# Six of the sixteen q/k transposes of an attention + experts kernel moved from TensorE to DMA by way of DRAM

## The chip, the cores and the metric

One core of one Trainium2 chip runs the whole program. The metric is the device time of one execution in microseconds (us). A set of runs alternates the kernel before with the kernels under test on the same chip. The chip was not the same in every set, so a kernel is compared with the kernel before of its own set. A profile comes from one execution of each kernel. TensorE is the matmul engine, VectorE and ScalarE the elementwise engines, GpSimd issues DMAs that cast, and SyncE ("SP") issues plain and transposing DMAs.

## The reference

```python
# q, k, v: [8 batches, 8 heads, 576 tokens, 64]; causal window of 128, ALiBi bias
scores = scale * q @ k.T + bias           # masked outside 0 <= i-j < 128
attn = softmax(scores); x = attn @ v      # -> x [4608 tokens, 512]
P = sinkhorn(exp(x @ w_gate), 8 rounds)   # [4608, 8 experts]
out = sum_e P[:, e] * (relu(x @ w1[e]) @ w2[e])
```

Three stages follow each other: attention (batches 0 to 7, about 10 to 192 us), the Sinkhorn rounds with some work of expert 0, and the experts (from about 230 us to the end). During attention TensorE also does work of expert 0 for token groups that are ready. The code calls that `fill`; the amount is fixed.

## The kernel before

A score matmul needs q and k with the head dimension on the partitions, so both are transposed. `load_qk` brings q and k in with a cast to fp16, `turn` rearranges a half batch on VectorE, and `tr_unit` transposes two heads with six TensorE transposes into one PSUM bank, from which ScalarE (k) or VectorE (q) copies them out. A tensor (the k or q of one batch) takes four such groups.

```python
def tr_unit(b, nm, j, swap=0):
    tt = turned[nm]
    psT = aps.tile([P, RT, RP], FP16, ..., tag="pmm", bufs=pmm)   # one PSUM bank
    for r in range(RT):                                           # RT = 6, RP = 96
        nc.tensor.matmul(out=psT[:, r, :],
                         lhsT=tt[:, r, 2 * Dh * jj : 2 * Dh * jj + 2 * Dh],
                         rhs=ident[0:RP, 0:RP], is_transpose=True, ...)
    copy = nc.scalar.copy if (nm == "k") != bool(swap) else nc.vector.tensor_copy
    copy(out=(KTs if nm == "k" else QTs)[b % 2][:, j, :]..., in_=psT...)

for i, (b, kb) in enumerate(blocks):        # five blocks of 128 tokens a batch
    if i < first_i: continue                # batches 0, 1, part of 2: a hand-written ORDER
    units = [(b + 1, nm, kb - 1) for nm in ("k", "q")]     # if kb >= 1: the NEXT batch
    pt0, mask0 = scores(b, kb, 0)           # score matmuls, exp on ScalarE
    gates(done); done = finish2(i - 2)      # transposes of x, store of x
    for u in units[: len(units) // 2]: tr_unit(*u)         # the k group
    fill(1)
    if turning: turn(b + 1, kb // 2, "k")
    mask0()
    pt1, mask1 = scores(b, kb, 1)
    xsbs[i - 1] = finish(i - 1)             # attention matmuls of the block before
    mask1(); fill(2)
    for u in units[len(units) // 2 :]: tr_unit(*u)         # the q group
    fill(1)
    if turning: turn(b + 1, kb // 2, "q")
    if kb == 0: load_v(b + 1)
    if kb == 3: load_qk(b + 2)
```

The score PSUM tile has one buffer, so the scores of one half can only be written when the exponential has read those of the half before.

The softmax here doesn't subtract the row's maximum and nothing guards it: scores larger than these inputs give would overflow.

## Time and profile before

| | |
|---|---|
| time, median | 1020.05 us (1018.93 to 1022.19, 4 runs) |
| profiled span | 1016.9 us |
| TensorE matmul busy | 98% of the span |
| batches 3 to 6, first score of 3 to first score of 7 | 72.6 to 165.4 us, 92.8 us |

The head of the page: span, and busy time of TensorE, its share and its instructions.

```profile
span 1016.9 us, 22579 instructions
...
PE 994.6 (98%) x9245; PEld 808.9 (80%) x9245; DVE 820.5 (81%) x1272; ACT 650.5 (64%) x1193; POOL 214.2 (21%) x224
```

The table by stretch, cut at the first score matmul of batches 3, 4, 5, 6 and 7. Columns: the stretch, its length, then busy us (and instructions) of TensorE, its weight loads, VectorE, ScalarE and GpSimd, then the granted clock, the mean DMA share and GB/s. (The prediction cut the same stage some 6 us later, from 78.5 us.)

```profile
core 0: us, PE busy (x) PEld busy (x) DVE busy (x) ACT busy (x) POOL busy (x), PEclk, DMA share, GB/s
72.60:96.70 24.10, 22.76 (x255) 12.71 (x252) 16.09 (x34) 16.20 (x29) 7.01 (x10) 1.00 0.81 101
96.70:119.80 23.10, 22.08 (x255) 12.45 (x252) 15.96 (x33) 15.76 (x29) 6.96 (x9) 1.00 0.85 101
119.80:142.00 22.20, 21.87 (x252) 12.28 (x250) 15.09 (x31) 16.01 (x28) 6.12 (x9) 1.00 0.87 104
142.00:165.40 23.40, 22.90 (x258) 12.75 (x256) 15.92 (x34) 16.69 (x30) 2.52 (x3) 1.00 0.35 60
```

TensorE is busy 89.6 of 92.8 us in batches 3 to 6; VectorE (63.1) and ScalarE (64.7) have room. The list of waits for these 92.8 us (line, tile, what it waited for, total us, times, longest) shows how little TensorE is held by others:

```profile
PE psS_2_0_1444 L265 <- ACT pt_1_1_1420 L276: 0.7, 1, 0.7
PE psS_3_0_1919 L265 <- ACT pt_2_1_1885 L276: 0.4, 1, 0.4
PE psS_3_0_1517 L265 <- ACT pt_2_1_1483 L276: 0.4, 1, 0.4
```

These are the three longest of nine, scores that wait for an exponential to free their PSUM tile; all nine sum to 3.0 us. Then one k group in the timeline (start, duration, engine, line, operation): six weight loads and six matmuls of L226, the first weight load of the next matmul 0.27 us after the group's first, and the copy out of PSUM on ScalarE.

```profile
87.58 0.33 PEld L226 LDWEIGHTS <-kp_1_1475 96*128 96x128 f16 x6
87.64 0.42 PE L226 MATMUL psT_k_2_1536<-ident,kp_1_1475 96*128 96x96 f16 x6
87.85 0.10 PEld L129 LDWEIGHTS <-w1t_122 128*128 128x128 f16 x1
...
88.17 0.65 ACT L235 COPY KT_75<-psT_k_2_1536 128x576 f16<-128x576 f16 x1
```

### The profile page before, as it was taken

The page shows a single profiled execution, that of the slowest core. Times are in us where ns is not written, and L with a number is a line of the kernel's source. Part 1 is how long each engine was busy: PE and PEld are TensorE (multiplying, and loading weights), DVE is VectorE, ACT ScalarE, POOL GpSimd, SP SyncE. Part 2 cuts the span into 40 slices and gives each one's busy share as a digit, 9 for nine tenths or more (in the row PEclk, how much of TensorE's full clock was granted, in tenths as well). Part 3 has the DMA queues.
Part 4 walks back from the last instruction along what each step waited for, and adds up shares of the span by engine and source line. Part 5 has one row for each costly group of instructions (what it writes and reads, how often), then busy time and mean ns, then how long its engine had stood idle before and what let it go on. Part 6 is the DMA issues. An engine that isn't in the chain of part 4 may idle for free. (4 is left out here: it accounts for less than half of the span.)

```text
span 1016.9 us, 22579 instructions
## 1 busy us (share of the span) xinstructions
PE 994.6 (98%) x9245; PEld 808.9 (80%) x9245; DVE 820.5 (81%) x1272; ACT 650.5 (64%) x1193; POOL 214.2 (21%) x224
## 2 busy tenths in 40 slices
PE   7899999999999999999999999999999999999997
PEld 4555555447888788888888888888888888888886
DVE  4677676587999897888888988888889988888886
ACT  6766776557999766666666556566656566666562
POOL 7423310110333221111112111111112112222222
PEclk9999999999999999999999999999999999999999
DMA  9997971391977874444447667444437645655546
GB/s 166 196 132 92 101 90 60 73 217 56 218 160 161 200 145 94 100 98 94 102 104 146 135 146 143 101 95 95 94 94 144 126 95 139 147 148 138 136 94 135
DMA packets 126936, 127.35 MB, mean 125 GB/s; under 512 B 44112, under 2 KB 104816, under 8 KB 126832
## 3 DMA queue, kind: packets, MB, share of 16 engines
q0 software_dynamic: 94784, 60.58, 43.2%
q1 hardware_dynamic: 31728, 65.07, 20.5%
q8 instruction: 72, 1.18, 0.5%
q10 hardware_dynamic: 320, 0.26, 0.1%
q14 instruction: 32, 0.26, 0.1%
HBM read 112.90 MB, written 16.66 MB: 127 GB/s over the span
## 5 line engine op out<-in xcount | busy, mean ns | idle before, releaser
L129 PEld LDWEIGHTS <-w1t_122 128*128 128x128 f16 x288 | 25.9, 97 | 26.9 <-issue 1.9
L743 PEld LDWEIGHTS <-w1t_3295 128*128 128x128 f16 x288 | 28.2, 98 | 5.1 <-issue 1.7
L743 PEld LDWEIGHTS <-w1t_3277 128*128 128x128 f16 x288 | 28.2, 98 | 4.6
L743 PEld LDWEIGHTS <-w1t_8419 128*128 128x128 f16 x288 | 28.1, 98 | 4.4 <-issue 0.3
L743 PEld LDWEIGHTS <-w1t_5217 128*128 128x128 f16 x288 | 28.1, 98 | 3.8 <-issue 0.3
L743 PEld LDWEIGHTS <-w1t_7883 128*128 128x128 f16 x288 | 28.2, 98 | 3.6 <-issue 0.3
L743 PEld LDWEIGHTS <-w1t_10819 128*128 128x128 f16 x288 | 28.2, 98 | 3.6 <-issue 0.3
L743 PEld LDWEIGHTS <-w1t_4035 128*128 128x128 f16 x256 | 25.1, 98 | 2.9
L204 POOL DMA_DIRECT2D vsb_79<-in_v_dram x20 | 17.1, 864 | 38.1 <-PE psN_1_1888 L318 5.9
L204 POOL DMA_DIRECT2D vsb_80<-in_v_dram x20 | 17.3, 870 | 34.8 <-PE psN_1_1486 L318 5.7
L576 POOL PARTITION_ALL_REDUCE ca_sb<-cs_sb x8 | 3.1, 389 | 63.0 <-DVE cs_sb L573 62.9
L265 PEld LDWEIGHTS <-KT_76 64*128 64x128 f16 (+1 forms) x160 | 5.4, 96 | 13.4 <-issue 12.1
L618 ACT ACTIVATE acc_lo<-acc_lo,Pe_sb 128x512 f32<-128x512 f32 (+1 forms) x24 | 14.8, 616 | 0.0
L265 PEld LDWEIGHTS <-KT_75 64*128 64x128 f16 (+1 forms) x160 | 5.2, 97 | 11.8 <-issue 10.4
L85 POOL DMA_DIRECT2D out_dram<-acc_lo x12 | 13.5, 1527 | 0.0
L343 PEld LDWEIGHTS <-xT 128*128 128x128 f16 x144 | 6.1, 96 | 5.1 <-issue 2.9
L871 POOL DMA_DIRECT2D acc_lo<-st_1_0_3878 x1 | 1.2, 1243 | 34.4 <-ACT st_1_0_3878 L870 34.4
L743 PEld LDWEIGHTS <-ws_2_4353 128*128 128x128 f16 x72 | 7.0, 98 | 1.5 <-issue 0.7
L743 PEld LDWEIGHTS <-ws_1_3597 128*128 128x128 f16 x72 | 7.0, 97 | 1.3
L85 POOL DMA_DIRECT2D out_dram<-acc_hi x6 | 5.7, 1575 | 9.7 <-DVE acc_hi L861 9.7
L898 DVE TENSOR_TENSOR acc_lo<-acc_lo 128x512 f32<-128x512 f32 x12 | 7.7, 685 | 0.0
L743 PEld LDWEIGHTS <-ws_6_10891 128*128 128x128 f16 x72 | 7.0, 98 | 0.8
(4175 smaller groups left out, 3566.4 us busy)
## 6 DMA issues: line engine op xcount, KB each, us to landing
xTd<-xT SPq DMA_DIRECT2D x9, 512.0 KB, 4.5
out_dram<-acc_lo SPq DMA_DIRECT2D x12, 256.0 KB, 5.3
vsb_79<-in_v_dram POOLq DMA_DIRECT2D x16, 128.0 KB, 5.8
vsb_80<-in_v_dram POOLq DMA_DIRECT2D x16, 128.0 KB, 5.8
out_dram<-acc_lo SPq DMA_DIRECT2D x12, 128.0 KB, 3.7
out_dram<-acc_lo POOLq DMA_DIRECT2D x12, 128.0 KB, 7.4
w1t_122<-in_moe_w_dram POOLq DMA_DIRECT2D x2, 512.0 KB, 11.3
w2t_130<-in_moe_w_dram POOLq DMA_DIRECT2D x1, 1024.0 KB, 16.4
```

Of the source, the lines that this page charges most:

```text
L85: eng.dma_start(out=out[t0 : t0 + n, c0:c1], in_=t[n * c : n * c + n], **kw)
L129: nc.tensor.matmul(out=psh, lhsT=w1t[:, dt, P * ft : P * ft + P], rhs=x[:, dt, :], start=(dt == 0), stop=(dt == NDT - 1),)
L204: nc.gpsimd.dma_start(out=vsb[0:nk, kb, :, 0:Dh], in_=v[b, :, k0 : k0 + nk, :].rearrange("h s d -> s h d"),)
L265: nc.tensor.matmul(out=ps[0:nk, hh, jj, 0:nq], lhsT=KT[rows, 2 * half + jj, k0 : k0 + nk], rhs=QT[rows, 2 * half + jj, k0 : k0 + nq], star ...
L343: nc.tensor.matmul(out=psG, lhsT=xT[:, dt, P * blk : P * blk + P], rhs=wg_sb[:, dt, :], start=(dt == 0), stop=(dt == NDT - 1),)
L576: nc.gpsimd.partition_all_reduce(ca_sb, cs_sb, P, bass_isa.ReduceOp.add)
L618: nc.scalar.mul(acc(blk)[:, c], acc(blk)[:, c], Pe_sb[:, 0, blk : blk + 1])
L743: nc.tensor.matmul(out=ps[:, f, :], lhsT=a[:, kt, f0 : f0 + P], rhs=b[:, kt, :], start=(m in (1, 5) and f == 0 and kt == 0), stop=(kt == 1 ...
L871: nc.gpsimd.dma_start(out=quad(self.g, rh, ch), in_=st, accum_op=ALU.add)
L898: tt(out=t, in0=t, in1=quad(g, 1, 1), op=ALU.add)
```

## The change

The intent is to take transposes off the bounding engine. For six tensors (k of batches 4 to 7, q of 5 and 7), a casting DMA writes fp16 to DRAM as [576 tokens, 512], and one transposing DMA on SP's queue reads it into the finished K or Q tile. `tr_unit` and `turn` are dropped for them.

```diff
+        by_dma = {("k", b) for b in range(4, B)} | {("q", b) for b in range(5, B, 2)}
+        d16 = {nb: nc.dram_tensor(..., [S, HD], FP16, kind="Internal").ap() for nb in sorted(by_dma)}
         def load_qk(b: int):
+            for nm, src in (("k", k), ("q", q)):
+                if (nm, b) in by_dma:
+                    nc.gpsimd.dma_start(
+                        out=d16[nm, b].rearrange("s (h d) -> s h d", d=Dh),
+                        in_=src[b].rearrange("h s d -> s h d"),
+                    )
...
-                    units = [(b + 1, nm, kb - 1) for nm in ("k", "q")]
+                    units = [(b + 1, n, kb - 1) for n in ("k", "q") if (n, b + 1) not in by_dma]
+                if kb == 1:
+                    for nm, t in (("k", KTs), ("q", QTs)):
+                        if (nm, b + 1) in by_dma:
+                            nc.sync.dma_start(
+                                out=t[(b + 1) % 2], in_=d16[nm, b + 1], transpose=True
+                            )
...
-                if turning:
+                if turning and ("k", b + 1) not in by_dma:
                     turn(b + 1, kb // 2, "k")
...          (the same for q)
```

More of the change, by code (lines that the diff above doesn't have):

```diff
@@ L184 @@
         raw: dict = {}
-        def load_qk(b: int):
+        by_dma = {("k", b) for b in range(4, B)} | {("q", b) for b in range(5, B, 2)}
+        d16 = {
+            nb: nc.dram_tensor(f"{nb[0]}16_{nb[1]}", [S, HD], FP16, kind="Internal").ap()
+            for nb in sorted(by_dma)
+        }
+        def load_qk(b: int):
+            for nm, src in (("k", k), ("q", q)):
[4 more added lines that the diff above has]
+                    )
             for half in range(2):
@@ L189, in load_qk @@
                 for nm, src in (("k", k), ("q", q)):
+                    if (nm, b) in by_dma:
+                        continue
                     t = asb.tile(
@@ L519 @@
                 fill(1)
-                if turning:
+                if turning and ("q", b + 1) not in by_dma:
                     turn(b + 1, kb // 2, "q")
```

## The prediction

> What bounds it now. The page gives TensorE matmuls 98% of the 1016.9 us span, clock 1.0. The change touches only attention; batches 3 to 6 run from 78.5 to 171.0 us. A table by stretch shows TensorE busy 88.6 of those 92.5 us, VectorE 62.5, ScalarE 64.6, and the DMA share 0.84, 0.83, 0.88, 0.22 in the four batches (it can pass 1: 0 to 50 us shows 1.49). The list of waits for 78 to 170 us finds TensorE held by other engines for some 4 us; most of the rest is a gap of about 0.42 us before many score matmuls. So TensorE's own stream bounds this stage.
>
> What goes. Six tensors (k of 4, 5, 6, 7, q of 5, 7), each four groups of six 96x96 transposes: 144 matmuls and weight loads. From a group's first matmul to the next instruction's first takes 0.26 us where no wait follows, up to 0.8 us where the gap before scores or a wait for ScalarE follows. All 24 groups give 24 x 0.26 = 6.2 us at least, about 9 us with what follows them, part of which stays. Off the critical path: 24 PSUM copies (0.65 us on ScalarE, 0.76 us on VectorE) and 12 turning copies on VectorE (0.55 us): about 10 us of ScalarE and 13 us of VectorE, which should remove some of the 4 us of waits.
>
> What comes. Casting loads from DRAM to DRAM: per tensor 4608 packets of 128 bytes written, in place of 1536 packets. The v loads use such packets at about 33 ns each, the old q/k loads about 85 ns, so estimated 16-engine time per tensor is 9.5 us against 8.1, if small writes to DRAM cost no more than to SBUF. Then one transposing DMA of 576 KB per tensor on SP's queue. The Trainium skill (DMA: Bandwidth & Descriptors, Latency and other measured facts) gives transposing DMAs 261 GB/s effective: an estimate of 2.3 us plus latency; this trace holds none.
>
> Critical path. The casting load is issued about two batches ahead (batch 6's q and k today at 101.4 us, batch 6 starting near 148). The transpose waits for that landing, for the store of x ahead of it in SP's queue, and for the scores of batch b-2 to release the K or Q buffer; then it has most of a batch, about 18 us, for one or two transposes. If each takes under 9 us no score matmul waits, and the gain is TensorE's: 6 to 9 us. The rest (Sinkhorn, experts) only starts earlier.
>
> Predicted: 1012.8 us, 0.7% faster; eight times in ten 1007.0 to 1019.0. Chances: faster by over 2% 0.03, within 2% 0.92, slower by over 2% 0.05. The removed TensorE work cannot reach 2% (20 us).
>
> What would show it. 144 fewer matmuls; the four batches, now 22.7, 23.8, 22.8 and 23.2 us, each shrink by 1 to 3 us, most in those preparing 5 and 7; later stretches keep their length; transposes land in under 9 us; no score matmul waits for a DMA; the DMA share nears or passes 1 in batches 3 to 5. Wrong if TensorE's busy time falls but the batches keep their length (another engine or the exp-mask chain sets the pace), or if the first scores of batch 5 or 7 wait on a transpose.
>
> What would make it wrong. Small writes to DRAM far dearer than 33 ns a packet, delaying v loads or x stores; transposes much slower than estimated, or holding up other DMAs: a stall of tens of us would make it slower. Or more gain, if freed VectorE and ScalarE time shortens the gaps before scores and attention.

## The result

The changed kernel took 1011.0 us (1010.1 to 1013.1, 4 runs) against 1020.05 us. The ratio is 0.9912, with a 95% interval of 0.9889 to 0.9934: 0.9% faster. A ratio here is the mean time of one kernel's runs over that of the other's runs of the same rounds, so it is not quite the ratio of the medians. The predicted 1012.8 us (1007.0 to 1019.0) holds it.

The page after:

```profile
span 1008.9 us, 22248 instructions
...
PE 988.7 (98%) x9101; PEld 802.6 (80%) x9101; DVE 809.1 (80%) x1252; ACT 642.0 (64%) x1177; POOL 219.1 (22%) x218
```

The same table by stretch, with the same cuts:

```profile
core 0: us, PE busy (x) PEld busy (x) DVE busy (x) ACT busy (x) POOL busy (x), PEclk, DMA share, GB/s
72.00:94.60 22.60, 21.54 (x231) 11.63 (x232) 15.11 (x32) 13.99 (x25) 8.77 (x7) 1.00 1.47 134
94.60:115.70 21.10, 19.85 (x207) 10.16 (x208) 12.40 (x26) 13.24 (x24) 7.77 (x8) 1.00 1.52 172
115.70:136.80 21.10, 20.77 (x225) 11.23 (x224) 13.47 (x28) 13.91 (x24) 7.89 (x7) 1.00 1.51 133
136.80:158.00 21.20, 20.75 (x210) 10.44 (x209) 12.20 (x27) 14.43 (x26) 2.43 (x3) 1.00 0.72 122
```

Batch by batch, 24.1, 23.1, 22.2, 23.4 us became 22.6, 21.1, 21.1, 21.2 us. All four sum to 86.0 in place of 92.8 us, and TensorE's busy time in them fell by the same amount, 89.6 to 82.9 us. What follows keeps its length: batch 7 with the tail of attention 27.1 and 27.1 us, the Sinkhorn stage 37.0 and 36.8 us, the experts 787.4 and 787.0 us. The start took 72.0 against 72.6 us; more on its scatter below. The DMA share in the first three rose from 0.81 to 0.87 before to about 1.5.

The waits of TensorE in batches 3 to 6:

```profile
PE psS_3_0_1837 L280 <- ACT pt_2_1_1813 L291: 0.7, 1, 0.7
PE psS_2_0_1432 L280 <- ACT pt_1_1_1408 L291: 0.7, 1, 0.7
PE psS_4_0_1902 L280 <- ACT pt_3_1_1873 L291: 0.5, 1, 0.5
```

No score matmul waits for a DMA. The waits for an exponential grew slightly, from a total of 1.9 us to 2.5 us with the shorter ones that are left out here. The transposing DMAs in the timeline of SP's queue (start, time that the issue took):

```profile
70.39 3.15 SPq L519 DMA_TRANSPOSE KT_75<-k_4  x1
91.52 0.52 SPq L461 DMA_DIRECT2D xTd<-xT  x1
92.14 3.11 SPq L519 DMA_TRANSPOSE KT_76<-k_5  x1
95.36 4.36 SPq L519 DMA_TRANSPOSE QT_78<-q_5  x1
...
136.03 2.50 SPq L519 DMA_TRANSPOSE KT_76<-k_7  x1
138.63 3.92 SPq L519 DMA_TRANSPOSE QT_78<-q_7  x1
```

And from issue to landing, first the six transposes, then the six casting loads:

```profile
DMA to landing us min/median/max: 6.0/7.1/7.9
```

```profile
DMA to landing us min/median/max: 8.1/9.4/11.0
```

The second transpose of batch 5 went out at 95.4 us, and the first scores of batch 5 are at 115.7 us.

### The profile page after: what moved, and what is told of

The parts are those of the page before. It is cut to its first block, busy times and chain, and to the rows that moved or that the text cites. A ratio compares the mean times of both kernels' runs of the same rounds, so it can differ in the third digit from the quotient of the medians.

```text
span 1008.9 us, 22248 instructions
## 1 busy us (share of the span) xinstructions
PE 988.7 (98%) x9101; PEld 802.6 (80%) x9101; DVE 809.1 (80%) x1252; ACT 642.0 (64%) x1177; POOL 219.1 (22%) x218
## 5 line engine op out<-in xcount | busy, mean ns | idle before, releaser
L219 POOL DMA_DIRECT2D vsb_79<-in_v_dram x20 | 17.1, 864 | 36.8 <-PE psN_1_1093 L333 7.0
```

The lines of the kernel that those rows point to most:

```text
L219: nc.gpsimd.dma_start(out=vsb[0:nk, kb, :, 0:Dh], in_=v[b, :, k0 : k0 + nk, :].rearrange("h s d -> s h d"),)
```

## The experiments

Lengths of batches are read off the first score matmul of each batch in each kernel's trace. For batches 3 to 6 they repeat to about 0.1 us (two profiles of the changed kernel: 86.04 and 86.06 us; two of q46_too: 85.20 twice), so they show differences that the total time, with its scatter, can't. "0+1" is batches 0 and 1 together, which do not repeat like this (37.9 and 41.3 us for the changed kernel), and in which only b3_too and the three kernels that reorder the start (b3_early, b3k_early, q46_fill) differ from the kernel before.

| kernel | ratio (95%) | median us | 0+1 | 2 | 3 | 4 | 5 | 6 | 3 to 6 |
|---|---|---|---|---|---|---|---|---|---|
| before | | 1020.05 | 38.6 | 24.0 | 24.1 | 23.1 | 22.2 | 23.4 | 92.8 |
| changed | 0.9912 (0.9889-0.9934) | 1011.0 | 37.9 | 24.0 | 22.6 | 21.1 | 21.1 | 21.2 | 86.0 |
| set 1: changed, again | 0.9932 (0.9914-0.9950) | 1012.1 | 41.3 | 24.0 | 22.6 | 21.1 | 21.1 | 21.2 | 86.1 |
| pe_back | 0.9985 (0.9970-1.0000) | 1017.56 | 38.8 | 24.0 | 24.1 | 22.7 | 22.2 | 22.9 | 91.9 |
| copies_back | 0.9943 (0.9928-0.9958) | 1013.86 | 39.0 | 24.0 | 22.6 | 21.2 | 21.9 | 22.1 | 87.8 |
| q46_too | 0.9915 (0.9899-0.9931) | 1010.57 | 37.7 | 24.0 | 22.1 | 21.2 | 20.7 | 21.3 | 85.2 |
| set 2: all_back | 1.0003 (0.9986-1.0021) | 1019.15 | 38.6 | 24.0 | 24.1 | 23.2 | 22.2 | 23.4 | 92.9 |
| twice | 0.9938 (0.9921-0.9955) | 1012.78 | 38.2 | 24.0 | 22.6 | 21.1 | 21.1 | 21.2 | 86.0 |
| mirror | 0.9941 (0.9923-0.9958) | 1012.78 | 38.1 | 24.0 | 23.1 | 21.2 | 21.8 | 21.2 | 87.3 |
| b3_too | 1.0016 (1.0000-1.0032) | 1020.66 | 37.7 | 29.4 | 23.7 | 21.2 | 20.7 | 21.3 | 86.8 |
| set 3: b3_early | 0.9939 (0.9924-0.9955) | 1011.39 | 38.1 | 21.5 | 22.1 | 21.2 | 22.7 | 22.3 | 88.3 |
| b3k_early | 0.9932 (0.9919-0.9945) | 1010.78 | 41.3 | 22.5 | 22.1 | 21.2 | 20.7 | 21.3 | 85.2 |
| q46_again | 0.9929 (0.9917-0.9940) | 1010.23 | 38.3 | 24.0 | 22.1 | 21.2 | 20.7 | 21.2 | 85.2 |
| set 4: q46_fill | 0.9912 (0.9899-0.9926) | 1009.5 | 37.6 | 24.0 | 22.1 | 21.2 | 20.7 | 21.3 | 85.2 |

The median of the kernel before was 1018.98, 1018.78, 1017.67 and 1018.68 us in sets 1 to 4.

### Theory and rival

Theory A: the gain is TensorE's own instruction time, about 0.28 us for each of 24 groups (6.8 us over 24). Rival B: the gain is the relief of ScalarE and VectorE, whose copies out of PSUM went too. Rival C, for going further: the DMA engines are at a limit.

**The changed kernel again, as yardstick of the set** (no edit).

> The changed kernel itself, unaltered, as the yardstick of this set of rounds. Both theories expect about 1011 us, ratio to the kernel before about 0.991, within 0.3%.

It measured 1012.1 us, ratio 0.9932, with 86.1 us in batches 3 to 6: as expected. Its runs fell into two groups, 1010.8 to 1011.0 us at a mean clock of 0.999 to 1.000 and 1013.2 to 1014.9 us at 0.996 to 0.997; see "the scatter".

**pe_back: the transposes alone put back.**

```diff
+            dummy = (nm, b) in by_dma
-                    lhsT=tt[:, r, ...],
+                    lhsT=ident[0:RP, :] if dummy else tt[:, r, ...],
+            if dummy:
+                return                       # no copy out of PSUM
-    units = [... if (n, b + 1) not in by_dma]
+    units = [(b + 1, n, kb - 1) for n in ("k", "q")]
```

> The changed kernel with its DMA transposes kept, plus the 144 transposes back on TensorE as dummies (identity in, PSUM out, nobody reads them, no copies on VectorE or ScalarE). Theory A (the gain is TensorE's own instruction time, 0.28 us for each of 24 groups): the loss of most of the gain, 1016.5 to 1020 us, ratio 0.997 to 1.000, and batches 3 to 6 back to 23 to 24 us each. Rival B (the gain is the relief of ScalarE and VectorE, whose copies no longer hold PSUM banks and whose queues are shorter): stays at 1010 to 1013 us.

The time went back to 1017.56 us and batches 3 to 6 to 91.9 us: 5.8 of the 6.8 us are lost with TensorE's transposes alone. Rival B, which expected 1010 to 1013 us, falls. The waits for an exponential fell back from 2.5 us to the 1.9 us of the kernel before, in the same view:

```profile
PE psS L283 <- ACT pt L294: 1.9, 5, 0.7
```

The 0.9 us that are left (92.8 - 91.9, in batches 4 and 6) are what the relief can be worth. The run all_back below, which has the real copies as well, is 1.0 us longer than this one and agrees.

**copies_back: the copies alone put back, as stand-ins.**

```diff
+            if (nm, b) in by_dma:            # in tr_unit: the copy without the transposes
+                copy = nc.scalar.copy if nm == "k" else nc.vector.tensor_copy
+                copy(out=fake_out..., in_=fake_in...)
+                return
-                if turning and ("k", b + 1) not in by_dma:
+                if turning:                  # turn() reads a constant for these; the same for q
...          (units again holds both tensors, as in pe_back; the fake tiles are two spare ones)
```

> The changed kernel plus stand-ins for the 24 copies (128x576, on the same engines at the same places, from a constant) and the 12 turning copies on VectorE, but no TensorE transposes. Theory A: no more than 1.5 us over the changed kernel (about 1011 to 1012.5 us). Rival B: the gain is lost, 1016 to 1020 us.

1013.86 us; batches 3 to 6 took 87.8, 1.7 us over the changed kernel. That is just past what theory A allowed, and far from rival B's loss. But the stand-in, which reads fp32, was too heavy on ScalarE (and a little light on VectorE, 654 ns against some 755). In the groups by line (line, engine, operation, tiles, shapes, count, busy us, mean ns) it took 1209 ns, where the real copy takes about 650:

```profile
L244 ACT CAST fake_out<-fake_in 128x576 f16<-128x576 f32 x16 | 19.3, 1209 | 0.9 <-DVE fake_out L244 0.8
```

The waits for an exponential, which runs on ScalarE, rose from 2.5 to 4.2 us in this run, which is the whole 1.7 us. So 1.7 us is probably an overstatement, and 0.9 us from the run before is the better figure for the relief.

**q46_too: q of batches 4 and 6 by DMA as well.**

```diff
-        by_dma = {("k", b) for b in range(4, B)} | {("q", b) for b in range(5, B, 2)}
+        by_dma = {(nm, b) for nm in ("k", "q") for b in range(4, B)}
```

> q of batches 4 and 6 transposed by DMA as well: 8 more groups off TensorE. Theory A with DMA slack left: 8 x 0.28 = 2.2 us faster than the changed kernel, 1008 to 1009.5 us, batches 3 and 5 shrinking by about 1 us each. Rival C (the DMA engines are at their limit, mean share about 1.5 in batches 3 to 5, and that is why these two were left out): no faster than the changed kernel, or slower, with score matmuls of batches 4 or 6, or attention matmuls, waiting for a DMA.

It was no slower (1010.57 us against 1012.1 us in the same set, intervals of the ratios that overlap), and no wait for a DMA appeared, so rival C has nothing for it here. But 8 more groups were worth 0.84 us in batches 3 to 6 (86.04 to 85.20 us), not the 2.2 us that theory A expected. The list of waits says where the rest went:

```profile
PE psS L280 <- ACT pt L291: 3.6, 7, 0.9
```

Scores waiting for an exponential rose from 2.5 to 3.6 us in total. A q group stands between the scores of one half and those of the next. Where no expert work is left to fill that place, taking the group away makes TensorE arrive before the exponential has freed the score PSUM tile. The trace shows it: in this run scores follow an attention matmul directly, with nothing between, at seven places, and the seven waits stand at just these; in the changed kernel there are two such places, in the kernel before none. At the undiluted price of a group that mirror gives below, 0.26 us, eight groups are worth 2.1 us, of which some 1.1 us came back as this wait.

**all_back: the engine work of the kernel before, with all the DMA traffic of the change beside it.**

```diff
-                    units = [... if (n, b + 1) not in by_dma]      (on top of the changed kernel)
+                    units = [(b + 1, n, kb - 1) for n in ("k", "q")]
+                in_=(w1ts[0][...] if (nm, b) in by_dma else raw.pop(...))      # turn() from a constant
+                out=(fake_out if (nm, b) in by_dma else (KTs ...)[...])        # copies to a spare tile
```

> The kernel before, in engine work (transposes, PSUM copies and turning copies all run, on data that is thrown away), with the six casting loads and six DMA transposes of the change beside it, whose results are used. If the added DMA traffic costs nothing on the critical path, as my prediction said: batches 3 to 6 take 92.8 us together as before (within 0.5), ratio 0.998 to 1.002. If the traffic delays v loads or others and the true saving of engine work is larger than the net gain: more than 93.3 us and over 1.002.

1019.15 us, ratio 1.0003, batches 3 to 6 at 92.9 us: the added DMA traffic is free here. The net gain is the whole value of the engine work taken away.

**twice: each transposing DMA issued twice, the second into a spare tile.**

```diff
+                            nc.sync.dma_start(out=spare, in_=d16[nm, b + 1], transpose=True)
```

> Every DMA transpose issued a second time, into a tile nobody reads, in the same queue right after the first: 12 transposes in place of 6. If they have the slack that I predicted (18 us, landing seen in 6 to 8 us), two tensors take about 16 us of issue and landing and batches 3 to 6 stay at 86.0 us together (within 0.5), ratio as the changed kernel. If the slack is smaller: the first scores of batch 5 or 7 wait for a DMA, and batches 4 and 6 lengthen by 1 us or more each.

Batches 3 to 6 took 86.0 us, to 0.01 us as the changed kernel; the ratio, 0.9938, lies in the changed kernel's range. SP's queue, for the four transposes that prepare batch 5:

```profile
92.56 3.17 SPq L520 DMA_TRANSPOSE KT<-k  x1
95.83 4.00 SPq L523 DMA_TRANSPOSE spare<-k  x1
99.93 3.12 SPq L520 DMA_TRANSPOSE QT<-q  x1
103.55 5.24 SPq L523 DMA_TRANSPOSE spare<-q  x1
```

The Q transpose went out at 99.9 us, 4.6 us later than in the changed kernel, and that costs nothing; the first scores of batch 5 come at 116 us. The K transpose of batch 6, behind these, took 11.7 us to land, and nothing waited for it either. The slack that the prediction counted on is there.

**mirror: q of 4 to 7 and k of 5 and 7, so k groups stay in place of q groups.**

```diff
-        by_dma = {("k", b) for b in range(4, B)} | {("q", b) for b in range(5, B, 2)}
+        by_dma = {("q", b) for b in range(4, B)} | {("k", b) for b in range(5, B, 2)}
-                for u in units[: len(units) // 2]:
+                for u in units[: (len(units) + 1) // 2]:      # k keeps its old place; second loop alike
```

> The mirror image of the choice: q of 4 to 7 and k of 5 and 7 by DMA, so that the k of 4 and 6 stay on TensorE in their old places, ahead of expert matmuls, and no q group stands ahead of a score matmul. The same 144 transposes go. Theory S (a group ahead of scores is cheap, since it fills the gap of some 0.3 us that stands before scores anyway, so q groups are worth about 0.13 us each and k groups about 0.3): batches 3 and 5 take about 23.6 and 21.7 us, the four 87.5 to 88.2 us. Theory D (the first group removed is worth more than the second, since less work between two score halves leaves them waiting for the exponential): 86.0 to 86.6 us as the changed kernel.

87.3 us, 1.28 us behind the changed kernel, though the same number of transposes went: place matters. It lies between the two theories, 0.2 us under S's range (87.5 to 88.2) and 0.7 us over D's (86.0 to 86.6), and S's mechanism is not what the trace shows. From an expert matmul's start to the next score matmul's it is 0.31 us where two expert matmuls are 0.22 us apart, so about 0.1 us of gap. From the last transpose of a q group to the scores it is 0.14 us where two transposes are 0.04 us apart: the same 0.1 us. A q group fills no gap. (These are medians over batches 3 to 6 in the trace of the kernel before.) What differs is D's wait, in the place that S named:

```profile
PE psS L280 <- ACT pt L291: 3.4, 6, 0.9
```

3.4 us of waiting for exponentials against 2.5 us accounts for some 0.9 of the 1.28 us; the rest is not settled. Against q46_too, which has nearly the same waits, the eight k groups that mirror keeps cost 87.32 - 85.20 = 2.1 us, or 0.26 us a group. That is the undiluted price of a group.

(The Trainium skill, TensorEngine Tiling (Array Packing), Key Properties, says that changing the tiling mode drains TensorE. Every score matmul here uses 64 of 128 rows; the 0.1 us before it agrees with that, though no run separates it from other causes.)

### Going further

**b3_too: k and q of batch 3 by DMA too.**

```diff
+        by_dma = {(nm, b) for nm in ("k", "q") for b in range(3, B)}
                 elif c == "v":
                     load_v(n[0])
+                    # batch 3's two transposing DMAs go here, in block 11 of the hand-written order;
+                    # its turn and tr_unit entries are skipped
```

> k and q of batches 3 to 7 all by DMA: 16 groups fewer on TensorE than the changed kernel, 8 of them in batch 2, whose casting loads go out about 40 us, when the DMA engines are busiest. At the worth that the last set showed (q of 4 and 6 together 0.84 us in batches 3 to 6, a pair of k and q about 2 us a batch) 2.8 us faster than the changed kernel: 1008 to 1010 us, ratio 0.988 to 0.991, batch 2 at 22 us in place of 23.96. If the casting loads of batch 3 come late in the crowded start: batch 2 or the first scores of batch 3 wait for DMA and it is no faster than the changed kernel.

It lost everything: 1020.66 us, no faster than the kernel before. The second alternative of the expectation came true. The list of waits from 30 to 100 us, SP's queue, and stretches of 2 us around the wait (same columns as above; the clock is the third number from the end):

```profile
PE psS L280 <- DMA QT<-q: 7.8, 1, 7.8
```

```profile
55.91 6.95 SPq L486 DMA_TRANSPOSE KT<-k  x1
62.98 7.74 SPq L486 DMA_TRANSPOSE QT<-q  x1
```

```profile
74.00:76.00 2.00, 0.00 (x0) 0.00 (x0) 0.00 (x0) 0.00 (x0) 0.00 (x0) 0.50 1.96 156
...
78.00:80.00 2.00, 2.00 (x9) 0.90 (x8) 1.10 (x2) 0.91 (x2) 0.00 (x0) 0.50 1.45 190
```

The transposes of batch 3 went out late, at 55.9 us, behind a store of x. They took 7 to 8 us each to issue and 14 us to land, where the same took 2.1 to 4.4 us and 6.0 to 8.2 us in the last batches, and the first scores of batch 3 waited 7.8 us, to 77.2 us. Worse, the granted clock was 0.50 from 73.9 to 80.7 us, so the first 3.5 us of work ran at half clock. That accounts for 23.7 us in batch 3 in place of 22.1.

**b3_early: the same, loads and transposes moved ahead in their queues.**

```diff
-        "... g1 l2 u1.3.1 ... s6.1 l3 "         (l3 = casting loads of batch 3)
+        "... g1 l2 l3 u1.3.1 ... s6.1 "
-        "... s9.1 m9.0 m9.1 ..."
+        "... s9.1 d3 m9.0 m9.1 ..."             (d3 = its transposing DMAs)
```

> k and q of 3 to 7 by DMA as in the run that lost 7.8 us to a wait for q of batch 3, but with the casting loads of batch 3 right after those of batch 2 (before the v loads of batch 2) and their transposes put into the queue right after the last scores of batch 1 (before a store of x that held them back to 55.9 us). If order in the queues caused that wait: the transposes go out near 47 to 50 us, the wait is under 1 us, batch 2 takes 22 to 22.5 us in place of 29.4, batches 3 to 6 85.2 us, the whole 1007 to 1010 us, ratio 0.987 to 0.991. If the crowded DMA engines caused it: the transposes still take 7 us or more each to issue, batch 2 still over 25 us or the v loads of batch 2 come late and batch 1 or 2 waits, and it is no faster than the changed kernel.

```profile
46.72 6.37 SPq L489 DMA_TRANSPOSE KT<-k  x1
53.20 6.49 SPq L489 DMA_TRANSPOSE QT<-q  x1
```

They went out at 46.7 us and the wait at batch 3 was gone: batch 2 took 21.5 in place of 29.4 us, and the eight groups of this batch alone are worth 24.0 - 21.5 = 2.5 us. So order in the queues had caused that wait; whether the loads or the transposes mattered more is not separated, since both moved. But these two still took over 6 us each to issue and 12 us to land. The later ones of this run took 5.4 to 8.5 us to issue, and the first scores of batch 6 waited:

```profile
PE psS L280 <- DMA QT<-q: 2.2, 1, 2.2
```

```profile
134.00:136.00 2.00, 0.10 (x2) 0.14 (x4) 0.86 (x2) 0.00 (x0) 0.87 (x1) 1.00 2.01 185
136.00:138.00 2.00, 2.00 (x15) 0.97 (x13) 1.03 (x2) 1.09 (x2) 0.00 (x0) 0.57 1.51 252
```

After a wait of 2.2 us the clock was 0.50 for 3.4 us, from 136.3 to 139.7 us: batches 5 and 6 gave back 3.0 us (88.3 against the 85.2 that was expected). Here the crowded DMA engines do show: in this run the casting loads of batches 4 to 7 took 15 to 22 us to land, against 8 to 13 us in q46_too, and the transposes' packets of 256 bytes took 35.1 ns each on average, against 23.6 ns. In total it was 1011.39 us, over the expected 1007 to 1010 us and not better than q46_again beside it. Why the DMAs stayed slow there, in batches whose DMA work is that of q46_too, is open.

**b3k_early: only k of batch 3.** The edit is that of b3_early with `by_dma = {("k", b) for b in range(3, B)} | {("q", b) for b in range(4, B)}`.

> The same with q of batch 3 left on TensorE: one transpose fewer in the crowded stretch. If order was the cause: batch 2 near 22.8 us, the whole 1008 to 1010.5 us, behind the run with both. If the crowd was the cause: half the load, wait of 0 to 3 us, about 1010 to 1013 us.

1010.78 us; batch 2 took 22.5 and batches 3 to 6 85.2 us, no wait for a DMA at batch 3. That is 1.5 us better than q46_again in batches 2 to 6. Its profiled run lost more than that in batches 0 and 1 (41.3 against 38.3 us), by the same fall of the clock as below. As a whole it can't be told from q46_again, and it does not decide between the two alternatives of its expectation: batch 2 fits the first, the whole the second.

**q46_again: q46_too once more, as yardstick of that set** (no new edit).

> k and q of 4 to 7 by DMA, the same kernel as before in this study, as the yardstick of this set: 1010.6 us, ratio 0.9915 within 0.2%, batches 3 to 6 85.2 us.

1010.23 us, ratio 0.9929, 85.2 us: within 0.2% as expected.

### The scatter, and a version with a reordered start

Runs of one kernel within a set scattered by 1.4 to 6.2 us (q46_fill, below, by less). The changed kernel's second profile, with a span of 1013.1 us and a mean clock of 0.996, has the same 86.1 us in batches 3 to 6, but 41.3 in place of 37.9 us in batches 0 and 1. Its wait list from 30 to 52 us, and stretches of 2 us:

```profile
PE psT_q L241 <- DVE qp L230: 3.5, 1, 3.5
```

```profile
38.00:40.00 2.00, 0.00 (x0) 0.00 (x0) 0.56 (x1) 1.01 (x2) 1.04 (x2) 0.97 1.31 203
...
42.00:44.00 2.00, 2.00 (x15) 1.29 (x13) 1.36 (x4) 0.64 (x1) 0.75 (x2) 0.50 2.35 158
44.00:46.00 2.00, 2.00 (x20) 1.03 (x19) 0.20 (x1) 1.22 (x3) 1.33 (x2) 0.50 2.05 173
```

TensorE stood 3.5 us, waiting for a rearranged half of q of batch 2 whose load came late; the clock was 0.50 from 39.9 to 46.7 us, some 5 us of it work. The profiled run of b3k_early shows the same with a wait of 3.1 us. In the run of the kernel before the same wait was 1.6 us, and the clock held:

```profile
PE psT_q_1_709 L226 <- DVE qp_0_680 L215: 1.6, 1, 1.6
```

The Trainium skill, TensorE: Matmul & The Clock Gate (Part 1: The HAM clock gate), gives half clock after an idle window of about 3.4 us, and full clock after a busy one. The runs agree with the two levels (0.50 and 1.00) and with 3.5 us tripping it; the 2.2 us above tripped it too. But in the profiles of q46_too and b3_too waits of 2.7 and 2.4 us in this same place left the clock at 1.00 (which the expectation below overlooks), so between 2.2 and 2.7 us the length of a wait alone does not decide. In the clock records of the traces the stretches at half clock between 10 us and the experts last 3.41 or 6.83 us, and the stretches at full clock before them 27.31, 61.44 and 116.05 us: 1, 2, 8, 18 and 34 times 3.413 us. So where a wait falls on such a grid may decide; no run tests that.

**q46_fill: two pieces of work moved ahead of the transposes that wait.**

```diff
-        "... m7.1 f f s8.0 U2.1.1 u2.1.1 x5 f s8.1 "
+        "... m7.1 f f s8.0 x5 f U2.1.1 u2.1.1 s8.1 "
+        by_dma = {(nm, b) for nm in ("k", "q") for b in range(4, B)}
```

> k and q of 4 to 7 by DMA, and besides, in batch 1, one transpose of x and one expert group's matmuls moved ahead of two transposes that wait for a late load of q of batch 2 (that wait was 3.5 us in the run of the changed kernel whose granted clock then fell to 0.50, and 0 to 1.6 us in runs at full clock). If the spread between runs of one kernel comes from this wait reaching the length at which the clock falls: about 1 us of work goes into the wait, it stays under 2.6 us, no run has a mean clock under 0.998, all runs lie within 1009 to 1011.5 us. If the clock falls for another reason: runs at 0.996 to 0.997 and 1012 to 1015 us still occur. Batches 3 to 6 stay at 85.2 us either way.

The first alternative of the expectation came true: all five runs lie between 1009.07 and 1009.78 us at clocks of 0.998 to 0.999, a spread of 0.7 us where q46_too had 3.6 and 2.0 in its two sets and the changed kernel 4.2 in set 1. Its wait list shows no wait of TensorE in that place. Five runs are few for this: of the eleven runs of the same kernel without the reordering (q46_too and q46_again) only two fell to 0.996 or 0.997. The two profiles with the wait and the half clock in them are the better evidence. It has the lowest median, 1009.5 us, but its ratio to the kernel before, 0.9912, is that of the changed kernel in its first set (0.9932 in its second), and the two were never in one set. So it is not shown to be faster.

## Why the prediction was right

- **"TensorE's own stream bounds this stage": right.** Putting the transposes alone back returned 5.8 of 6.8 us.
- **"24 x 0.26 = 6.2 us at least, about 9 us with what follows": right.** Batches 3 to 6 lost 6.8 us, and a group's undiluted price measured 0.26 us. But TensorE's transposes alone were worth 5.8 us, a little under the floor; the 6.8 us hold some 0.9 us of relief. The two profiled spans differ by 8.1 us: 6.8 us there, 0.6 us in the start and 0.7 us behind attention, neither of which the change touches. The medians differ by 9.1 us; the last 1 us is within the scatter. In set 1 the same two kernels differed by 6.9 us, so some 2 of the 9.1 us are luck in the scatter, and the ratio of set 1, 0.9932, is nearer to what the change does.
- **"Each shrink by 1 to 3 us, most in those preparing 5 and 7": right.** They shrank by 1.5, 2.0, 1.0 and 2.2 us.
- **Relief of ScalarE and VectorE "should remove some of the 4 us of waits": small at best.** The relief was worth about 0.9 us (inferred from the runs with dummies, not measured alone), but the main wait, for exponentials, rose from 1.9 to 2.5 us: TensorE arrives earlier. Some waits for freed PSUM banks went.
- **Casting loads at 33 ns a packet: right.** Packets of 128 bytes, 43% of them now to DRAM and the rest v loads, averaged 32.2 ns over the trace after; with the v loads at the 32.9 ns of the trace before, that leaves about 31 ns for the casts to DRAM. The loads landed in 8.1 to 11.0 us.
- **"An estimate of 2.3 us plus latency" for a transpose: too low for what a kernel sees.** The Trainium skill (DMA: Bandwidth & Descriptors, Latency and other measured facts) gives 261 GB/s, for a case with a non-contiguous middle dimension; here 576 KB took 6.0 to 7.9 us from issue to landing, which is 75 to 98 GB/s with all latency in it. It did no harm because the argument only needed under 9 us, and the doubled transposes, of which one took 11.7 us, showed that even that was not tight.
- **The warnings were well placed.** Transposes much slower than estimated, and a stall, are what b3_too ran into in the crowded start, not the change itself.

## What to carry to other kernels

Here work taken from the bounding engine and given to DMA was worth its full time, because the data was needed a batch later; check the slack by doubling the transfer, and the price by putting the work back as dummies. Such gains dilute: where no other work was left between two dependent steps, part of the next removal turned into a wait for the step between (here the exponential). Be wary of extending it into a stretch whose DMA engines are already crowded, and look at the granted clock: waits of TensorE of 2.2, 3.1 and 3.5 us were followed by 3.4 to 6.8 us of half clock here, though others of 2.4 and 2.7 us were not.

## What the Trainium skill lacked or had wrong

- DMA: Bandwidth & Descriptors has no issue time, on trn2, of a transposing DMA of this size from DRAM. In the changed kernel SP was held 2.5 to 4.4 us for each 576 KB transpose, and 5.4 to 8.5 us in crowded stretches of b3_too and b3_early, against 0.5 us for a plain 512 KB store.
- The same page's 261 GB/s is no guide to latency beside other traffic: 6.0 to 7.9 us for 576 KB from issue to landing in the change.
- The same page says that transfers under 512 bytes are read-modify-write and below line rate, but not whether DRAM is then a dearer target than SBUF. Casting writes of 128 bytes to DRAM took about 31 ns a packet (worked out above), no more than the 33 ns of the v loads into SBUF.
- TensorE: Matmul & The Clock Gate gives an idle window of about 3.4 us. A wait of 2.2 us was followed by a clock of 0.50 in one run, while waits of 1.1, 1.6, 2.4 and 2.7 us were not.
- No page says how much of a removed TensorE group comes back as a wait; here 0.26 us a group became about 0.1 us (0.84 us over 8) where the scores' PSUM tile had one buffer.
